# Output copies over two blocks, earlier ranks and row numbers, and a PReLU joined from PSUM, in one FFN

## The chip, the cores and the metric

One NeuronCore of one Trainium2 chip runs the whole program. The metric is the device time of one execution in microseconds (us), taken as the median of several runs. Besides these runs there is one execution under the hardware profiler, from which all rows below come. Engines are named as the profile does: PE is TensorE's matmuls, PEld its weight loads, DVE is VectorE, ACT is ScalarE, POOL is GpSimd, SP is SyncE, which issues most DMAs.

## The reference, cut to what matters

Three stages follow each other, all in float32:

```python
attn = softmax_with_cluster_mask(q, k) @ v          # 2 x 8 heads x 768 x 64
x = attn.transpose(0, 2, 1, 3).reshape(1536, 512)

h = x @ w_in                                        # 512 -> 2048
g = np.maximum(h, 0.0) + alpha * np.minimum(h, 0.0) # PReLU, alpha per column of h
x = g @ w_out                                       # 2048 -> 512

out = x.copy()                                      # then a routed FFN:
e = argmax(x @ w_gate); p = softmax(x @ w_gate)[e]  # 8 experts, one per row
out[x @ w_skip > 0] += p * (relu(x @ w1[e]) @ w2[e])
```

The change lies in the middle stage, the FFN with the PReLU, and in the routing of the first half of its rows.

## The kernel before, in words

Instructions run on each engine in the order in which the Python program emits them (`manual_schedule`); engines wait for each other only through data and through buffers that come free. A float32 product is made from three passes: every operand is split into a rounded high part and a low part (`wh`, `wl` of weights, `xh`, `xl` and `gh`, `gl` of activations), and PE adds high x high, high x low and low x high.

**The FFN** (`ffn`, from L588) works on two halves of the 1536 rows, `gi` = 0 and 1, six row tiles (`GT`) each. In a half a loop runs over 16 blocks `f` of 128 hidden columns. A block has a first layer, `hidden(gi, f)`, and a second layer, `second(gi, f - 1)`, of the block in front of it. The first layer works in two chunks of 384 rows (`c` = 0, 1): PE fills an `h` tile (12 matmuls), a PReLU makes `m` from it, ACT rounds `m` to `gh` (L656) and DVE subtracts to `gl` (L658). The `h` tiles share two PSUM buffers (`ps_h`); ranks (`rk`) and row numbers (`sv`) take their PSUM tiles from the same two. The second layer adds 18 matmuls of 512 columns, three passes over the six row tiles, into six accumulators `ys`. Those are the six buffers of `ps_y`, one PSUM bank each; together with `ps_h` they fill PSUM. The accumulators of half 1 are allotted in `second(1, 0)`, in the first pass over the six tiles, and take over the buffers of half 0 in turn.

**The PReLU** has three forms. The first two blocks of half 0 run beside the last tiles of attention and are made by `blocks()` with `act=True` ("the ACT blocks", four chunks): ACT writes Relu(-h) to `gt` and Relu(h) to `gm`, both from PSUM, and DVE joins them, `gt * nalpha + gm`, with all operands in SBUF (L643 to L645). Half 1 has ACT write Relu(-h), then ACT scale it by `nalpha` (L649, L650), and DVE join max(h, 0) from PSUM with it (L651). The other blocks of half 0 do it on DVE alone (L653, L654). During half 0, weights of later blocks are converted from int64 words by ACT, DVE and POOL (L560 to L568), and POOL makes most `wl`; in half 1 POOL is nearly idle.

**Between the halves** `evac(i)` copies accumulator `i` to SBUF with ACT (L688) and issues two DMAs on SP's queue, to `y1d` and to the output (L689, L690). Three copies are emitted in front of block 0 of half 1 and three behind its first chunk. `after(c)` runs behind each chunk; it also emits set-up constants on DVE and, from block 1, the gate products `gateb` of half 0's rows.

**In half 1's loop** each block first splits weights (`split`: an ACT cast L616 and a DVE subtraction L617), then runs `hidden(1, f)`, then `second(1, f - 1)` up to f = 12 (`TAIL` = 4: the second layers of blocks 12 to 15 come behind the loop, in `tail`). Behind the second layer come steps tied to a block's number: at f = 10 `route1` (choice of the expert, L880 to L890, and running counts `Ms`, L932, all on DVE), at f = 11 `route2` (softmax weight) and `ranks` (three small matmuls `rk`, L940 to L944, which read `M` and `Ms`, then positions on DVE), at f = 12 the first half of `first_tile` (DVE), at f = 13 its second half (six small matmuls `sv`, L968, and `gi0` on DVE) and the gather of rows on POOL's queue. Expert weights are also split here in pieces (`wsp.hi` on ACT, `wsp.lo` on DVE): at f = 6 to 9, and four pieces of a second part at f = 10 and 11.

Of the kernel before, what the change touches and what calls it, by code (L numbers as in the profile page):

```python
# [8 lines left out]
F32 = mybir.dt.float32  # L9
# [6 lines left out]
AF = mybir.ActivationFunctionType  # L16
ALU = mybir.AluOpType
# [3 lines left out]
P = 128  # L21
# [559 lines left out]
def ffn(tc, A, cst, xs, xp, y1d, R, cv, W32, fw, ps_h, cvt, more):  # L581
# [5 lines left out]
    nc = tc.nc  # L587
# [3 lines left out]
    GT = NTT // 2  # L591
    GN = GT * P
    HC = GN // 2
    alpha, nalpha = cst["alpha"], cst["nalpha"]
# [25 lines left out]
    def hidden(gi, f, eng, after, between=lambda: None):  # L620
        for _ in hiddens(gi, f, eng, after, between):
            pass

    def hiddens(gi, f, eng, after=lambda c: None, between=lambda: None, act=False, mid=lambda c: None):
        xh, xl = xs[gi]
        wh, wl = ws.pop((f, 0))
        if gi == 1 and NF - TAIL <= f < NF - 2:
            gh, gl = over["xh"].pop(0), over["xh"].pop(0)
        else:
            gh = fw.tile([P, GN], F32R, tag="gh", name="gh")  # L630
            gl = fw.tile([P, GN], F32R, tag="gl", name="gl")
        for c in range(2):
            o = slice(c * HC, (c + 1) * HC)
            h = ps_h.tile([P, HC], F32, tag="h", name="h")
            for i, (a, x) in enumerate(((wh, xh), (wh, xl), (wl, xh))):
                for k in range(KD):
                    nc.tensor.matmul(h, lhsT=a[:, k * P:(k + 1) * P], rhs=x[:, k, o], start=(k == 0 and i == 0), stop=(k == KD - 1 and i == 2))  # L637
                if i < 2:
                    yield
            m = fw.tile([P, HC], F32, tag="gm", name="gm")  # L640
            if act:
                t = fw.tile([P, HC], F32, tag="gt", name="gt", bufs=1)
                nc.scalar.activation(t, h, AF.Relu, scale=-1.0)  # L643
                nc.scalar.activation(m, h, AF.Relu)
                nc.vector.scalar_tensor_tensor(out=m, in0=t, scalar=nalpha[:, f:f + 1], in1=m, op0=ALU.mult, op1=ALU.add)  # L645
            elif gi == 1:

                t = fw.tile([P, HC], F32, tag="gt", name="gt", bufs=1)
                nc.scalar.activation(t, h, AF.Relu, scale=-1.0)  # L649
                nc.scalar.activation(t, t, AF.Copy, scale=nalpha[:, f:f + 1])  # L650
                nc.vector.scalar_tensor_tensor(out=m, in0=h, scalar=0.0, in1=t, op0=ALU.max, op1=ALU.add)  # L651
            else:
                nc.vector.tensor_scalar(out=m, in0=h, scalar1=0.0, scalar2=alpha[:, f:f + 1], op0=ALU.min, op1=ALU.mult)  # L653
                nc.vector.scalar_tensor_tensor(out=m, in0=h, scalar=0.0, in1=m, op0=ALU.max, op1=ALU.add)  # L654
            mid(c)
            nc.scalar.copy(gh[:, o], m)  # L656
            between()
            eng.tensor_tensor(out=gl[:, o], in0=m, in1=gh[:, o].bitcast(F32), op=ALU.subtract)  # L658
            after(c)
            if c == 1:  # L660
                gs[f] = (gh, gl)
            yield
# [22 lines left out]
    def evac(i):  # L685
        y = ys.pop(i)
        b = wk.tile([P, DM], F32, tag="yb", name="yb", bufs=6)
        nc.scalar.copy(b, y)  # L688
        nc.sync.dma_start(out=y1d[i * P:(i + 1) * P, :DM], in_=b)  # L689
        nc.sync.dma_start(out=A["out"][i * P:(i + 1) * P, :], in_=b)  # L690
        yb[i] = b
# [24 lines left out]
    def route1(t0, nt):  # L716
        ds[t0] = choose(nc, R, wk, LG[:, t0:t0 + nt], t0, nt)
        counts(nc, R, t0, nt)
# [22 lines left out]
    for n, _ in enumerate(blocks()):  # L741
        for _ in range(TODO[n] if n < len(TODO) else 0):
            next(conv2, None)
        if n in SPL:
            f, o = SPL[n]
            split(f, o, nc.gpsimd)
        yield
    wk, ck, ps_y, wsp, slot, last, even, xg, setup = more()
# [4 lines left out]
    for f in range(2, NF):  # L753
        split(f, 1, nc.gpsimd)

        def after(c):
            if c == 0:
                split((f + 1) % NF, 0, nc.gpsimd)
            else:
                convert(f + 2)  # L760
# [21 lines left out]
    for f in range(NF):  # L782
        if f > 0:
            if f < NF - 1:
                split(f + 1, 0, nc.vector)
            split(f, 1, nc.vector, 1)
        if f == 0:
            for i in range(GT // 2):
                evac(i)

        def after(c):
            if f == 0:
                if c == 0:
                    for i in range(GT // 2, GT):
                        evac(i)
                for _ in range(8):
                    next(consts, None)
                return
            for _ in range(2):
                next(consts, None)  # L800
            do(WORK[c])

        def do(n):
            for _ in range(n if f > 0 else 0):
                if work:
                    fn, args = work.pop(0)
                    fn(*args)

        hidden(1, f, nc.vector, after, lambda: do(1))
        if 0 < f <= NF - TAIL:  # L810
            second(1, f - 1)
        if f == 1:
            for c in range(2):
                wsp.load(0, c)
        if f == 2:
            wsp.even[0] = even(0)
        if f == 10:
            route1(0, GT)
        elif f == 11:
            route2(0, GT)  # L820
            for c in range(2, NPC):
                wsp.load(0, c)
            ranks(nc, R, wk, ps_h, 0, GT, "h")
        elif f == 12:
            oh = ck.tile([P, GT, P], F16, tag="ct", name="poh0")
            row0 = first_tile(nc, R, oh, wk, ps_h, "h", GT)
            next(row0)
        elif f == 13:
            next(row0)
            gather_rows(nc, xg, y1d[:GN], R["gi0"])  # L830
        for c, i in ((0, f - 6),) if 6 <= f < 10 else ((1, 2 * f - 20), (1, 2 * f - 19)) if f in (10, 11) else ():

            if i == 0:
                slot()
                wsp.take(0, c)
            wsp.hi(0, c, 512 * i, 512 * (i + 1))
            wsp.lo(0, c, nc.vector, 512 * i, 512 * (i + 1))
            if i == 3:
                wsp.load(1, c)
# [7 lines left out]
    for n in range(GT):  # L847
        i = GT + n
# [15 lines left out]
        if n < 4:  # L864
            c, o = divmod(n, 2)
# [8 lines left out]
def choose(nc, R, wk, lg, t0, nt):  # L874

    M, nd = R["M"], R["nd"]
    ts = slice(t0, t0 + nt)
    l8 = lg[:, :, :NE]
    mx = wk.tile([P, nt], F32, tag="rmx", name="rmx", bufs=1)
    nc.vector.tensor_reduce(out=mx, in_=l8, axis=AX.X, op=ALU.max)  # L880
    nc.vector.tensor_scalar(out=nd[:, ts], in0=lg[:, :, NE], scalar1=0.0, scalar2=FAR, op0=ALU.is_le, op1=ALU.mult)
    d = wk.tile([P, nt, NE], F32, tag="rd8", name="rd8", bufs=1)
    nc.vector.tensor_tensor(out=d, in0=l8, in1=mx.unsqueeze(2).to_broadcast([P, nt, NE]), op=ALU.subtract)

    q = wk.tile([P, nt, NE], F32, tag="rq8", name="rq8", bufs=1)
    nc.vector.scalar_tensor_tensor(out=q, in0=d, scalar=0.0, in1=R["ew"].unsqueeze(1).to_broadcast([P, nt, NE]), op0=ALU.is_equal, op1=ALU.mult)
    m2 = wk.tile([P, nt], F32, tag="rm2", name="rm2", bufs=1)
    nc.vector.tensor_reduce(out=m2, in_=q, axis=AX.X, op=ALU.max)
    nc.vector.tensor_tensor(out=m2, in0=m2, in1=nd[:, ts], op=ALU.add)
    nc.vector.tensor_tensor(out=M[:, ts], in0=q, in1=m2.unsqueeze(2).to_broadcast([P, nt, NE]), op=ALU.is_equal)  # L890
    return d
# [43 lines left out]
def ranks(nc, R, wk, ps, t0, nt, tag):  # L935
    M, Ms = R["M"], R["Ms"]
    ts = slice(t0, t0 + nt)
    rk = ps.tile([P, nt + 1, NE], F32, tag=tag, name="rk")
    rv = rk.rearrange("p t e -> p (t e)")
    nc.tensor.matmul(rv[:, :nt * NE], lhsT=R["tri"], rhs=M[:, ts].rearrange("p t e -> p (t e)"), start=True, stop=False)  # L940
    nc.tensor.matmul(rv[:, :nt * NE], lhsT=R["ones"], rhs=Ms[:, ts].rearrange("p t e -> p (t e)"), start=False, stop=True)
    if t0 == 0:

        nc.tensor.matmul(rk[:, nt], lhsT=R["ones"], rhs=Ms[:, nt], start=True, stop=True)  # L944
        d = wk.tile([P, 1], F32, tag="rdl", name="rdl", bufs=1)
        nc.vector.tensor_scalar(out=d, in0=rk[:, nt, 0:1], scalar1=-1.0, scalar2=float(P), op0=ALU.mult, op1=ALU.add)
        nc.vector.scalar_tensor_tensor(out=d, in0=d, scalar=0.0, in1=R["p0"], op0=ALU.max, op1=ALU.mult)
        nc.vector.tensor_tensor(out=Ms[:, nt, 0:1], in0=Ms[:, nt, 0:1], in1=d, op=ALU.add)
    for step in positions(nc, R, wk, rk[:, :nt], t0, nt):
        step()  # L950
# [689 lines left out]
```

## Time and profile before

| | us |
|---|---|
| median of 3 runs | 743.99 |
| lowest and highest run | 743.09, 745.3 |
| the profiled execution's own time | 744.96 |
| span of the profiled execution, first to last instruction | 743.2 |

The profiled execution is 0.97 us longer than the median, and 1.76 us of it lie outside the span. The rows further down are of two kinds. A row of a group has: line, engine, operation, output<-input, shapes, count, then busy us and mean ns of one, then idle time of the engine in front of the group and what ended it. A row of a timeline has: start in us from the span's start, duration in us, engine, line, operation, output<-input, how many instructions are merged (x), and in brackets the engine's idle time before it with the instruction that ended the wait.

### The profile page before, as it was taken

How to read it: one execution, taken by the hardware profiler on the slowest of the kernel's cores; microseconds unless marked ns; L12 is line 12 of the kernel's file. 1: busy time of each engine (PE TensorE's matmuls, PEld its weight loads, DVE VectorE, ACT ScalarE, POOL GpSimd, SP SyncE). 2: the span in 40 equal slices, each digit the busy share in tenths (PEclk: the TensorE clock that was granted, in tenths of full speed). 3: DMA queues.
4: the chain of work that ended last, by engine and by line, in shares of the span. 5: the costliest groups of instructions: out<-in, count | busy, mean ns of one | idle time of the engine just before them, and what ended most of it. 6: DMA issues, size and time to landing. Idle time of an engine off the chain costs nothing. (4 is left out here: it accounts for less than half of the span.)

```text
span 743.2 us, 11665 instructions
## 1 busy us (share of the span) xinstructions
PE 712.3 (96%) x4030; PEld 625.6 (84%) x4030; DVE 572.1 (77%) x1102; ACT 475.7 (64%) x914; POOL 365.0 (49%) x302
## 2 busy tenths in 40 slices
PE   8999999999999989999999999998989999999993
PEld 5988989988999878888888989988868888888872
DVE  5989888899988888888856899874478877775731
ACT  5879889797899855454536555556427767565630
POOL 4549769678684576666660000000128837482101
PEclk9999999999999999999999999999999999999997
DMA  7967665874663063334107000151629978685000
GB/s 207 228 164 178 130 152 142 198 183 96 155 136 103 0 227 114 114 133 149 73 0 283 1 1 0 58 169 36 235 63 395 395 263 284 254 290 221 17 10 18
DMA packets 45105, 109.21 MB, mean 147 GB/s; under 512 B 9723, under 2 KB 25531, under 8 KB 39665
## 3 DMA queue, kind: packets, MB, share of 16 engines
q1 hardware_dynamic: 38544, 72.01, 34.8%
q0 software_dynamic: 6496, 36.40, 13.4%
q8 instruction: 34, 0.56, 0.3%
q14 instruction: 31, 0.25, 0.1%
HBM read 74.78 MB, written 10.10 MB: 114 GB/s over the span
## 5 line engine op out<-in xcount | busy, mean ns | idle before, releaser
L339 DVE TENSOR_TENSOR etl<-pt,eth 128x384 fp32r<-128x384 f32 x192 | 101.9, 550 | 17.2 <-ACT eth L338 15.0
L338 ACT CAST eth<-pt 128x384 fp32r<-128x384 f32 x192 | 91.2, 489 | 20.5 <-PE pt L336 20.3
L336 PE MATMUL pt<-ident,e 128*128 128x128 f32 x576 | 93.9, 273 | 0.8 <-DVE etl L339 0.7
L318 DVE TENSOR_REDUCE nm<-s 128x1 f32<-128x768 f32 x96 | 90.6, 945 | 3.3 <-PE s L305 3.0
L1110 POOL DMA_INDIRECT xg<-y1d,gi x16 | 27.5, 1718 | 131.2 <-DVE gi L969 115.0
L325 ACT ACTIVATE e<-s,nm 128x768 f32<-128x768 f32 x96 | 87.6, 913 | 5.8 <-DVE nm L318 5.5
L656 ACT CAST gh<-gm 128x384 fp32r<-128x384 f32 x60 | 30.8, 514 | 85.0 <-DVE gm L654 58.9
L336 PEld LDWEIGHTS pt<-ident,e 128*128 128x128 f32 x576 | 73.2, 140 | 8.9 <-DVE etl L339 2.4
L658 DVE TENSOR_TENSOR gl<-gm,gh 128x384 fp32r<-128x384 f32 x60 | 49.9, 832 | 23.3 <-ACT gh L656 23.3
L354 PE MATMUL px<-etl,vh 128*64 128x384 f32 (+1 forms) x192 | 66.0, 370 | 1.7 <-DVE etl L339 1.6
L1374 DVE TENSOR_TENSOR wl<-raw,wh 128x2048 fp32r<-128x2048 f32 (+2 forms) x28 | 48.8, 1755 | 15.5 <-ACT wh L1370 15.5
L637 PE MATMUL h<-xh,wh 128*128 128x384 f32 x256 | 56.6, 343 | 3.7 <-DVE gm L651 3.1
L637 PE MATMUL h<-xh,wl 128*128 128x384 f32 x256 | 56.9, 343 | 1.5 <-DVE wl L617 1.0
L302 PE MATMUL s<-AB 128*128 128x384 f32 x192 | 57.3, 379 | 0.5
L637 PE MATMUL h<-xl,wh 128*128 128x384 f32 x256 | 55.7, 339 | 0.0
L568 POOL TENSOR_TENSOR pre<-ct,pre 128x512 int32<-128x512 int32 x26 | 37.2, 1450 | 36.3 <-DVE ct L566 36.3
L356 PE MATMUL px<-eth,vh 128*128 128x384 f32 x160 | 54.0, 337 | 0.0
L637 PEld LDWEIGHTS h<-xh,wh 128*128 128x128 f32 x256 | 45.7, 189 | 7.4 <-DVE gm L651 3.5
L1232 POOL DMA_INDIRECT out_dram<-o,si x16 | 22.1, 1381 | 60.4 <-DVE o L1227 27.3
L305 PE MATMUL s<-CD 128*128 128x384 f32 x192 | 49.3, 337 | 1.7 <-DMA CD<-st 1.0
L637 PEld LDWEIGHTS h<-xh,wl 128*128 128x128 f32 x256 | 45.0, 190 | 5.0 <-POOL wl L617 3.7
L1370 ACT CAST wh<-raw 128x2048 fp32r<-128x2048 f32 (+2 forms) x28 | 41.3, 1480 | 11.6 <-PE yo L1141 11.6
(337 smaller groups left out, 1831.3 us busy)
## 6 DMA issues: line engine op xcount, KB each, us to landing
AB<-RL SPq DMA_DIRECT2D x32, 384.0 KB, 5.1
raw<-in_wall_dram SPq DMA_DIRECT2D x12, 1024.0 KB, 8.0
raw<-in_w_in_dram SPq DMA_DIRECT2D x16, 512.0 KB, 4.1
raw<-in_w_out_dram SPq DMA_DIRECT2D x16, 512.0 KB, 4.7
Tp<-in_qkT_dram SPq DMA_DIRECT2D x16, 384.0 KB, 3.7
CD<-RL SPq DMA_DIRECT2D x16, 384.0 KB, 6.4
vt<-in_v_dram SPq DMA_DIRECT2D x8, 384.0 KB, 6.2
y1d<-yb SPq DMA_DIRECT2D x12, 256.0 KB, 3.7
```

The lines of the kernel that those rows point to most:

```text
L302: nc.tensor.matmul(s[:, u, :384], lhsT=AB[:, 0, t * P:(t + 1) * P], rhs=AB[:, 1, ks], start=True, stop=False)
L305: nc.tensor.matmul(s[:, u, :384], lhsT=CD[:, 0, t * P:(t + 1) * P], rhs=CD[:, 1, ks], start=False, stop=True)
L318: nc.vector.tensor_reduce(out=nm, in_=s[:, :, :384], axis=AX.XY, op=ALU.max, negate=True)
L325: nc.scalar.activation(e.rearrange("p (u c) -> p u c", u=2), s[:, :, :384], AF.Exp, bias=nm, accum_out=den[:, i % 3:i % 3 + 1])
L336: nc.tensor.transpose(pt[:, i2], e[:, kt * P:(kt + 1) * P], ident)
L338: nc.scalar.copy(eh, pt)
L339: lows[u] = lambda: nc.vector.tensor_tensor(out=etl[:, 3 * u:3 * u + 3, q * P:(q + 1) * P], in0=pt, in1=eh.bitcast(F32), op=ALU.subtract)
L354: nc.tensor.matmul(px[:m], lhsT=vh[:, kt, :m], rhs=etl[:, kt], start=False, stop=False)
L356: nc.tensor.matmul(px, lhsT=vh[:, kt, :], rhs=eth[:, kt], start=False, stop=(kt == NT - 1))
L637: nc.tensor.matmul(h, lhsT=a[:, k * P:(k + 1) * P], rhs=x[:, k, o], start=(k == 0 and i == 0), stop=(k == KD - 1 and i == 2))
L658: eng.tensor_tensor(out=gl[:, o], in0=m, in1=gh[:, o].bitcast(F32), op=ALU.subtract)
L1374: eng.tensor_tensor(out=lo[:, a:b], in0=self.src(t, c)[:, a:b], in1=hi[:, a:b].bitcast(F32), op=ALU.subtract)
```

## The change

- The six output copies of half 0 are spread: two in front of block 0 of half 1, one behind each chunk of block 0, one behind each chunk of block 1.
- `ranks` moves from behind `route2` at f = 11 to right behind `route1` at f = 10.
- `first_tile`'s first half moves from f = 12 to f = 11, its second half from f = 13 to f = 12, between the first layer of block 12 and the second layer of block 11; the gather of rows moves to f = 12.
- The four pieces of the second part of expert weights move from f = 10 and 11 to f = 11 and 12, with their buffer and the load that follows them.
- The ACT blocks use the PReLU of half 1: DVE joins max(h, 0), read from PSUM, with the scaled Relu(-h).

```diff
             m = fw.tile([P, HC], F32, tag="gm", name="gm")
-            if act:
-                t = fw.tile([P, HC], F32, tag="gt", name="gt", bufs=1)
-                nc.scalar.activation(t, h, AF.Relu, scale=-1.0)
-                nc.scalar.activation(m, h, AF.Relu)
-                nc.vector.scalar_tensor_tensor(out=m, in0=t, scalar=nalpha[:, f:f + 1], in1=m, op0=ALU.mult, op1=ALU.add)
-            elif gi == 1:
+            if act or gi == 1:
 
                 t = fw.tile([P, HC], F32, tag="gt", name="gt", bufs=1)
                 nc.scalar.activation(t, h, AF.Relu, scale=-1.0)
...
         if f == 0:
-            for i in range(GT // 2):
+            for i in range(2):
                 evac(i)
 
         def after(c):
+            if f < 2:
+                evac(2 + 2 * f + c)
             if f == 0:
-                if c == 0:
-                    for i in range(GT // 2, GT):
-                        evac(i)
                 for _ in range(8):
                     next(consts, None)
                 return
...
         hidden(1, f, nc.vector, after, lambda: do(1))
+        if f == 12:
+            next(row0)
         if 0 < f <= NF - TAIL:
             second(1, f - 1)
...
         if f == 10:
             route1(0, GT)
+            ranks(nc, R, wk, ps_h, 0, GT, "h")
         elif f == 11:
             route2(0, GT)
             for c in range(2, NPC):
                 wsp.load(0, c)
-            ranks(nc, R, wk, ps_h, 0, GT, "h")
-        elif f == 12:
             oh = ck.tile([P, GT, P], F16, tag="ct", name="poh0")
             row0 = first_tile(nc, R, oh, wk, ps_h, "h", GT)
             next(row0)
-        elif f == 13:
-            next(row0)
+        elif f == 12:
             gather_rows(nc, xg, y1d[:GN], R["gi0"])
-        for c, i in ((0, f - 6),) if 6 <= f < 10 else ((1, 2 * f - 20), (1, 2 * f - 19)) if f in (10, 11) else ():
+        for c, i in ((0, f - 6),) if 6 <= f < 10 else ((1, 2 * f - 22), (1, 2 * f - 21)) if f in (11, 12) else ():
```

## Rows read from the trace of the kernel before

**Rows 1.** The page's first part: busy time, share, instructions of each engine.

```profile
PE 712.3 (96%) x4030; PEld 625.6 (84%) x4030; DVE 572.1 (77%) x1102; ACT 475.7 (64%) x914; POOL 365.0 (49%) x302
```

**Rows 2.** Groups of instructions by line, whole span: the PReLU's operations and the subtraction.

```profile
L658 DVE TENSOR_TENSOR gl<-gm,gh 128x384 fp32r<-128x384 f32 x60 | 49.9, 832 | 23.3 <-ACT gh L656 23.3
...
L650 ACT ACTIVATE gt<-gt,nalpha 128x384 f32<-128x384 f32 x32 | 19.7, 617 | 1.0
...
L649 ACT ACTIVATE gt<-h 128x384 f32<-128x384 f32 x32 | 15.7, 489 | 23.0 <-PE h L637 23.0
...
L654 DVE SCALAR_TENSOR_TENSOR gm<-h,gm 128x384 f32<-128x384 f32 x28 | 15.6, 557 | 1.0
...
L645 DVE SCALAR_TENSOR_TENSOR gm<-gt,nalpha,gm 128x384 f32<-128x384 f32 x4 | 5.3, 1324 | 0.1
```

**Rows 3.** Timeline of DVE in half 0, first PReLU instruction of two successive blocks.

```profile
281.15 0.61 DVE L653 TENSOR_SCALAR gm<-h,alpha 128x384 f32<-128x384 f32 x1
...
289.66 0.61 DVE L653 TENSOR_SCALAR gm<-h,alpha 128x384 f32<-128x384 f32 x1
```

**Rows 4.** Timeline of POOL in the same block.

```profile
283.58 2.89 POOL L617 TENSOR_TENSOR wl<-pre,wh 128x512 fp32r<-128x512 f32 x2
```

**Rows 5.** Timeline of DVE in and behind the ACT blocks.

```profile
253.97 1.36 DVE L645 SCALAR_TENSOR_TENSOR gm<-gt,nalpha,gm 128x384 f32<-128x384 f32 x1
...
271.44 1.28 DVE L566 SCALAR_TENSOR_TENSOR ct<-raw,ct 128x512 int32<-128x512 int32 x2
```

**Rows 6.** Timeline of ACT in the ACT blocks, the first chunk's rounding.

```profile
255.36 0.51 ACT L656 CAST gh<-gm 128x384 fp32r<-128x384 f32 x1 [2.11 <-DVE gm L645]
```

**Rows 7.** Timeline of PE in and behind the ACT blocks: fourth chunk, then block 2.

```profile
258.89 0.97 PE L637 MATMUL h<-xh,wh 128*128 128x384 f32 x4 [0.48 <-ACT gm L644]
...
268.94 0.96 PE L637 MATMUL h<-xh,wl 128*128 128x384 f32 x4 [1.03 <-DVE wl L617]
```

**Rows 8.** Timeline of ACT, blocks 0 and 1 of half 1: copies, casts, rounding.

```profile
395.86 1.56 ACT L688 COPY yb<-y 128x512 f32<-128x512 f32 x3
...
400.02 0.61 ACT L616 CAST wh<-w32a 128x512 fp32r<-128x512 f32 x1
...
404.72 0.51 ACT L656 CAST gh<-gm 128x384 fp32r<-128x384 f32 x1 [0.69 <-DVE gm L651]
```

**Rows 9.** Timeline of DVE, block 0 of half 1: last constant, second chunk's join.

```profile
397.55 0.43 DVE L1432 TENSOR_TENSOR low<-iota 128x256 bf16<-128x256 f32 x1
398.48 0.56 DVE L651 SCALAR_TENSOR_TENSOR gm<-h,gt 128x384 f32<-128x384 f32 x1 [0.51 <-ACT gt L650]
```

**Rows 10.** Timeline of PE: block 1's second chunk, then the second layer's first two passes.

```profile
399.10 0.97 PE L637 MATMUL h<-xh,wh 128*128 128x384 f32 x4 [1.29 <-DVE gm L651]
...
401.31 1.55 PE L673 MATMUL y<-wh,gh 128*128 128x512 f32 x6
402.70 1.53 PE L673 MATMUL y<-wl,gh 128*128 128x512 f32 x6
```

**Rows 11.** Timeline of PE, block 10: last pass of the second layer.

```profile
478.83 1.52 PE L673 MATMUL y<-wh,gl 128*128 128x512 f32 x6
```

**Rows 12.** Timeline of DVE behind block 10: the running counts.

```profile
480.62 1.14 DVE L932 TENSOR_TENSOR Ms<-Ms,M 128x8 bf16<-128x8 bf16 x6
```

**Rows 13.** Timeline of PE: row numbers behind block 13's first layer, then block 14.

```profile
501.15 0.30 PE L968 MATMUL sv<-rs,poh 128*128 128x1 f16 x6
503.28 1.49 PE L637 MATMUL h<-xh,wh 128*128 128x384 f32 x4 [1.83 <-DVE gm L651]
...
507.03 0.86 PE L637 MATMUL h<-xh,wh 128*128 128x384 f32 x4
```

**Rows 14.** Windows: PE, PEld, DVE, ACT, POOL busy, then PEclk, DMA share, GB/s.

```profile
398.00:400.00 2.00, 0.90 (x5) 0.91 (x6) 0.94 (x2) 1.38 (x3) 0.00 (x0) 1.00 1.00 370
...
505.00:507.00 2.00, 2.00 (x8) 2.00 (x7) 0.64 (x2) 0.00 (x0) 1.09 (x1) 0.52 0.08 16
```

**Rows 15.** Timeline of ACT, block 14 of half 1: first chunk's Relu.

```profile
507.29 0.49 ACT L649 ACTIVATE gt<-h 128x384 f32<-128x384 f32 x1 [2.48 <-PE h L637]
```

## The prediction, made before the change was timed

> **What bounds the kernel now.** The page's first part comes first: PE is busy 96% of the span [rows 1], so a gain must come from a wait of PE, or from an engine that paces PE in a stage. The groups by line give the PReLU's prices: the join from SBUF costs 1324 ns on DVE, the one from PSUM 557 [rows 2]. The timelines then show who paces PE where.
>
> In half 0, DVE paces. The first PReLU instruction starts at 281.15 and, one block later, at 289.66 [rows 3]: a period of 8.51 us, which DVE fills with its own work and with waits for ACT's rounding, while POOL makes weights beside it [rows 4]. In the ACT blocks DVE goes from one instruction to the next from 253.97 to 272.72 [rows 5], and ACT stands 2.11 us for DVE's join [rows 6]. PE waits 0.48 us there for an `h` tile, and in block 2 1.03 us for a low part of weights that DVE made late [rows 7].
>
> In half 1, PE paces, but for two waits. ACT makes three accumulator copies in one go behind the first chunk [rows 8], the second chunk's join comes late [rows 9], and PE waits 1.29 us for that `h` tile [rows 10]. Behind block 10's second layer [rows 11] DVE makes the running counts [rows 12], with PE a block away from needing them. Behind block 13's first layer the row numbers take an `h` buffer, so block 14 waits 1.83 us for the other one [rows 13]; the granted clock is then 0.52, the lower level of 1.2 GHz, though after the 1.29 us it had stayed at 1.00, 2.4 GHz [rows 14]. ACT stands idle 2.48 us before block 14's first chunk reaches it [rows 15].
>
> **The PReLU in the ACT blocks: -2.6 us.** Four joins of 1324 ns become four of 557: 4 x 0.767 = 3.07 us of DVE time saved [rows 2]. That the join from PSUM keeps its price beside a busy POOL is seen in half 0: L654 has a PSUM operand and its mean over 28 is 557, although POOL works then [rows 4]; L658, with two SBUF operands, has a mean of 832 [rows 2]. In return ACT scales (617 ns) where it made a second Relu (489): 4 x 0.13 = 0.5 us, which lengthens the way to the join. Net: 3.07 - 0.5 = 2.6. As DVE has no pause from 253.97 to 272.72 and paces the rest of half 0, I count all of that. PE pays a little on the way: the `h` tile is now held until DVE's join, so its wait at 258.89 grows (some 0.5 us by the joins' new places), but what PE waits for behind it, ACT's work and DVE's weights, comes earlier by more. Bounds: 3.07, and nothing.
>
> The Trainium skill (VectorE: DVE Perf Modes, "The perf-mode tier table" and "Rules for kernel authors") speaks against this edit: an operand in PSUM gives at best the slowest rate, which a two-tensor float32 operation has in SBUF too, and for several operations it advises copying out of PSUM first. By it this term would be nothing, and the sum +4.6; the rows show the PSUM form at less than half the price, so I keep -2.6.
>
> **The copies: +3.6 us, and +1.7 from the clock.** One price is given up: behind block 0's first chunk stands one copy (1.56 / 3 = 0.52) instead of three, and ACT is 1.04 earlier. DVE cannot follow so far, since its constants run to 397.55 + 0.43 = 397.98; the join moves from 398.48 to 398.0 [rows 9]. PE's second chunk of block 1 starts at 398.6 instead of 399.1, and second(1, 0) at 400.8 instead of 401.3: -0.5 [rows 10].
>
> But the wait that I see coming is longer. All six accumulators of half 0 must be copied before half 1's can take their banks, in the first pass of second(1, 0). Before, that was done at 395.86 + 1.56 = 397.4 [rows 8], and PE went through the pass without a stop. Now the fifth copy stands behind the first chunk's rounding in block 1, the sixth behind the second chunk's. ACT reaches the casts of block 1 (400.02 is the second [rows 8]) at the same time as before: the 0.5 it won goes to the fourth copy. The fifth copy delays what follows by another 0.4 to 0.5, so the rounding at 404.72 [rows 8] comes at about 405.05; the sixth starts 0.4 later and takes 0.6: done at 406.05. PE has six tiles in a pass of 1.39 us (401.31 to 402.70 [rows 10]): it does four from 400.8, waits for the fifth until 403.3 and for the sixth until 406.1. The second pass starts at 406.3 instead of 402.70: +3.6 net of the 0.5. Queued behind are the rest of the second layer and block 2. From below: even with ACT idle at once, Relu, scaling, join, rounding and copy take about 3 us (0.49 + 0.62 + 0.56 + 0.5 + 0.6 [rows 2, 8]) behind the last matmul, against 1.1 us of PE's work: +2 less 0.5.
>
> PE stands for some 4 us of 4.4 here. After 1.83 us the clock fell, and three groups of four matmuls took 3.75 us (503.28 to 507.03 [rows 13]) where at 2.4 GHz they take 2.1: 1.66 lost. I add 1.66; bounds nothing and twice that.
>
> The SP queue gets six copies' twelve DMAs later, and behind them the loads for blocks 6 on, over 30 us ahead of their use: nothing.
>
> **The ranks: +1.6 us.** They now follow `route1` at once. The second layer's last pass starts at 478.83 [rows 11] and block 11 would start one pass later, at 480.2. The counts end at 480.62 + 1.14 = 481.76 [rows 12]; nothing in the change brings them forward, as they hang on block 10's own second chunk. So PE stands from 480.35 to 481.8, with block 11's first layer queued behind: 1.6. The idle time of 1.45 lies nearer to 1.29, where the clock stayed, than to 1.83, where it fell [rows 13, 14]; I take no fall. Bounds: 1.6 and 1.6 + 1.66.
>
> **The row numbers: -2.3 us.** In front of second(1, 11) the same buffer turn is harmless: 4 us of second layer lie between. The wait of 1.83 and the 1.66 of low clock go, 3.5 together, but ACT comes next: per chunk it has Relu, scaling, a wait for the join, and rounding, and blocks 13 and 14 add two casts each without a second layer as cover. ACT can move up by no more than the 2.48 it stood idle [rows 15], and DVE's joins, which free `h` for block 15, move with it; PE will stand about 1.1 us in front of block 15. The six small matmuls take 0.2 to 0.3 [rows 13] where they now stand. 2.48 - 0.2 = 2.3. Bounds: 0.6 (the clock falls in the new wait) and 3.5.
>
> **Moved at no price.** Two weight pieces per block leave f = 10 and come to f = 12, about 1.3 us of DVE a block (two 512-column operations [rows 5]) and 1.0 of ACT. At f = 12 they take the place of `first_tile`'s DVE work, which goes to f = 11 where the ranks left; second layers hide them. Uncovered, a block would cost 1.3. The gather, alone on POOL's queue, goes out a block earlier; its rows are read in the tail.
>
> **Sum.** -2.6 + 3.6 + 1.66 + 1.6 - 2.3 = +2.0. From the profiled 744.96 that is 746.9; from the median, 0.97 lower, **746.0**. A difference of 0.3%, 2.2 us, is about what a measurement of this kernel can tell from no change: 741.8 to 746.2. My forecast is just inside it.
>
> **Rivals.**
> 1. *Slower: the clock falls in the ranks' wait too.* It decides if 1.45 us are enough. For it: 1.83 were; against: 1.29 were not [rows 13, 14]. +2.0 + 1.66 = +3.6: 747.6. Chance 0.22.
> 2. *Slower: the join from PSUM brings nothing*, because its bank is held longer or the first layer's wait eats it. +4.6: 748.6. Against it: L654's price beside POOL, and DVE without a pause [rows 2, 4, 5]. Chance 0.13. By the Trainium skill's rule named above (VectorE: DVE Perf Modes) it would come out so.
> 3. *No change: the clock stays up or recovers within the stand* at second(1, 0). +0.3: 744.3. Chance 0.13.
> 4. *Faster: the first pass does not wait for the late copies*, so the spreading does what it says and no more (-0.5): -2.6 - 0.5 + 1.6 - 2.3 = -3.8, 740.2. Against it: six live accumulators in six buffers. Chance 0.10.
>
> The forecast has 0.42. Its own spread, about 1 us either way, leaves some 0.25 of that within 0.3% and 0.17 above. With rival 3 and the edges of the others: faster 0.11, same 0.43, slower 0.46. The range, 742.0 to 749.0, leaves out rival 4 and the two highest bounds together.
>
> **What would show it.** DVE's join of the ACT blocks near 557 ns, and block 3 of half 0 some 2.6 us earlier: right; a join above 1 us: wrong. PE waiting for `yb<-y` copies in second(1, 0), over 3 us, with a lower clock behind it: right; no such wait: wrong, and the kernel is faster. PE waiting 1.4 us for `Ms` before block 11, with the clock at 1.00: right. No wait in front of block 14, a new one near 1.1 us for a join in front of block 15: right.

## The result, and the profile after

Over 20 runs of each kernel, the changed kernel takes 748.49 us in the median (747.29 to 750.28), the kernel before 743.92 (742.78 to 749.26). The ratio is 1.0053 with a 95% interval of 1.004 to 1.0065: 3.9 us slower, 3.0 to 4.8; the two medians lie 4.57 apart, within that interval. The forecast was 746.0, +2.0, with a range to 749.0. The profiled execution after took 747.79, with a span of 746.0 against 743.2 before: +2.8. One reason why this pair differs by less than the runs is given further down, under the row numbers.

The page's first part answers [rows 1]: PE is busy 4.2 us longer for the same 4030 matmuls.

```profile
PE 716.5 (96%) x4030; PEld 628.9 (84%) x4030; DVE 570.5 (76%) x1102; ACT 475.9 (64%) x914; POOL 366.5 (49%) x302
```

These 4.2 us are not the change's: 3.0 of them lie ahead of the FFN's first product (242.16 busy instead of 239.13), which comes at 247.15 here and came at 247.19 before. From the first product of half 1 to that of block 2 PE is busy 2.8 longer (15.59 instead of 12.77), from block 13 to the tail 1.6 less (13.08 instead of 14.68), and both of these are in the main the clock, as the windows further down show. Next, the groups by line that answer to [rows 2]. L646 was L651 before and has taken the four chunks of the old L645; numbers behind L640 are 5 or 6 lower now.

```profile
L645 ACT ACTIVATE gt<-gt,nalpha 128x384 f32<-128x384 f32 x36 | 22.2, 617 | 1.2
L646 DVE SCALAR_TENSOR_TENSOR gm<-h,gt 128x384 f32<-128x384 f32 x36 | 20.0, 555 | 24.3 <-ACT gt L645 24.3
```

All 36 joins from PSUM have a mean of 555 ns, the four new ones among them. What became of the DVE time that they save is seen in DVE's timeline behind the ACT blocks, first before (its rows go with [rows 5]), then after:

```profile
270.10 0.75 DVE L562 TENSOR_SCALAR ct<-ct 128x512 f32<-128x512 f32 x2
270.77 0.75 DVE L564 TENSOR_SCALAR ct<-ct 128x512 int32<-128x512 int32 x2
```

```profile
253.96 0.54 DVE L646 SCALAR_TENSOR_TENSOR gm<-h,gt 128x384 f32<-128x384 f32 x1
...
266.94 2.21 DVE L562 TENSOR_SCALAR ct<-ct 128x512 f32<-128x512 f32 x2
269.07 0.75 DVE L564 TENSOR_SCALAR ct<-ct 128x512 int32<-128x512 int32 x2
```

The pair of conversions L562 starts 3.16 us earlier than before, then takes 2.21 us instead of 0.75, and the next pair is only 1.70 earlier (269.07 against 270.77). That 1.7 reaches the end of half 0: the first product of half 1 starts at 389.64 instead of 391.37.

In half 1 the groups of PE's waits name the losses. The columns are: engine, output and line, what it waited for, us in total, times, longest.

```profile
PE y L668 <- ACT yb L683: 3.6, 2, 2.2
...
PE rk L935 <- DVE Ms L926: 1.0, 2, 0.8
```

The first line is new: 3.6 us in which the second layer waits for output copies. PE's timeline shows where, and answers to [rows 10]; the windows (PE, PEld, DVE, ACT, POOL busy, then granted clock, DMA share, GB/s) show the clock.

```profile
398.95 1.09 PE L668 MATMUL y<-wh,gh 128*128 128x512 f32 x4
401.49 0.50 PE L668 MATMUL y<-wh,gh 128*128 128x512 f32 x1 [1.46 <-ACT yb L683]
404.15 0.80 PE L668 MATMUL y<-wh,gh 128*128 128x512 f32 x1 [2.16 <-ACT yb L683]
404.75 2.76 PE L668 MATMUL y<-wl,gh 128*128 128x512 f32 x6
407.31 2.37 PE L668 MATMUL y<-wh,gl 128*128 128x512 f32 x6
409.51 0.88 PE L637 MATMUL h<-xh,wh 128*128 128x384 f32 x4
```

```profile
399.00:401.00 2.00, 1.04 (x5) 0.52 (x3) 1.78 (x6) 1.34 (x4) 0.00 (x0) 1.00 0.50 186
401.00:403.00 2.00, 0.50 (x1) 0.19 (x1) 1.67 (x10) 1.45 (x3) 0.00 (x0) 0.82 0.36 136
403.00:405.00 2.00, 0.85 (x2) 0.75 (x3) 2.00 (x11) 1.51 (x3) 0.00 (x0) 0.50 0.36 134
405.00:407.00 2.00, 2.00 (x6) 1.52 (x6) 1.68 (x5) 0.00 (x0) 0.00 (x0) 0.50 1.12 303
407.00:409.00 2.00, 2.00 (x6) 1.53 (x5) 0.00 (x0) 0.00 (x0) 0.00 (x0) 0.50 0.86 270
409.00:411.00 2.00, 2.00 (x12) 1.90 (x11) 0.58 (x1) 0.62 (x1) 0.00 (x0) 0.98 1.01 406
```

Four of six tiles run, then PE waits for the fifth copy and again for the sixth. The clock falls within this stand (the time in which PE waits), not behind it, and the two passes behind it run at 1.2 GHz (0.50), the second all but its end: 2.76 and 2.37 us where a pass had taken 1.53 [rows 10]. The second pass starts 2.05 later than before (404.75 against 402.70), block 2 4.08 later (409.51 against 405.43).

Last, PE's timeline around the ranks and the row numbers, which answers to [rows 13]:

```profile
484.71 0.18 PE L934 MATMUL rk<-M,tri 128*128 128x48 bf16 x1 [0.27 <-DVE M L884]
485.69 0.18 PE L935 MATMUL rk<-Ms,ones 128*128 128x48 bf16 x1 [0.80 <-DVE Ms L926]
...
498.49 0.30 PE L962 MATMUL sv<-rs,poh 128*128 128x1 f16 x6
...
512.37 0.97 PE L637 MATMUL h<-xh,wh 128*128 128x384 f32 x4 [0.86 <-DVE gm L646]
```

The ranks stand in front of block 11, which starts at 485.91 instead of 480.19: 5.72 late where block 10 was 4.08 late, so +1.64. The row numbers run without a wait; block 14 starts at 507.02 without one either, and a wait of 0.86 stands in front of block 15. From block 13's start to the tail it is 13.94 us (502.83 to 516.77) instead of 16.51 (496.96 to 513.47).

### The profile page after: what moved, and what is told of

Its sections match the earlier page's. It is cut to its first block, busy times and chain, and to the rows that moved or that the text cites. A ratio compares the mean times of both kernels' runs of the same rounds, so it can differ in the third digit from the quotient of the medians.

```text
span 746.0 us, 11665 instructions
## 1 busy us (share of the span) xinstructions
PE 716.5 (96%) x4030; PEld 628.9 (84%) x4030; DVE 570.5 (76%) x1102; ACT 475.9 (64%) x914; POOL 366.5 (49%) x302
## 5 line engine op out<-in xcount | busy, mean ns | idle before, releaser
L1104 POOL DMA_INDIRECT xg<-y1d,gi x16 | 23.9, 1496 | 130.3 <-DMA raw<-in_wall_dram 114.1
L651 ACT CAST gh<-gm 128x384 fp32r<-128x384 f32 x60 | 30.8, 514 | 81.9 <-DVE gm L649 59.8
```

## The experiments

**Each part alone.** Four kernels make one part of the change each, in the kernel before.

The PReLU:

```diff
-            if act:
...
-            elif gi == 1:
+            if act or gi == 1:
```

> Only the PReLU of the ACT blocks is changed, all else as before. Theory: DVE paces half 0, the four joins fall from 1324 to about 550 ns, but DVE's conversion for block 3 then meets POOL's last attention work and gives part back: half 1 starts 1.7 us earlier than before, time -1.7 us (ratio 0.9977). Rival one (the prediction's own sum): nothing is given back, -2.6 us. Rival two (an operand in PSUM brings nothing): within 0.5 us of before, and joins above 1 us.

Ratio to before 0.9977 (0.9953 to 1.0001), 743.16 us over 12 runs: about -1.7, in an interval from -3.5 to +0.1. From the first product of the FFN to the first one of half 1 it is 142.5 us (247.74 to 390.27), against 144.2 before (247.2 to 391.4) and 142.5 after. The pair L562 is slow here too. DVE's timeline:

```profile
267.49 2.20 DVE L562 TENSOR_SCALAR ct<-ct 128x512 f32<-128x512 f32 x2
```

By the trace the part is worth 1.6 to 1.7 us by itself, so the shortfall belongs to it and not to its neighbours in the change.

The copies:

```diff
-            for i in range(GT // 2):
+            for i in range(2):
                 evac(i)
...
+            if f < 2:
+                evac(2 + 2 * f + c)
             if f == 0:
-                if c == 0:
-                    for i in range(GT // 2, GT):
-                        evac(i)
```

> Only the six output copies are spread over blocks 0 and 1 of half 1. Theory: PE stands for the fifth and sixth copy in the first pass of the second layer, the second pass starts 3.6 to 3.8 us later than before counted from the start of half 1, and the clock falls to its lower level and takes 1 to 2 us more: +4.8 to +5.8 us in all. Rival: the copies are not waited for, -0.5 us. Second rival: the wait is there and the clock stays up, +3.7 us.

Ratio 1.0081 (1.0053 to 1.011), 752.08 us over 7 runs: about +6.0 (+3.9 to +8.2), more than the whole change costs and a little more than expected. PE's timeline has the two waits, and the first product of block 2:

```profile
403.80 0.51 PE L673 MATMUL y<-wh,gh 128*128 128x512 f32 x1 [1.45 <-ACT yb L688]
406.46 0.79 PE L673 MATMUL y<-wh,gh 128*128 128x512 f32 x1 [2.15 <-ACT yb L688]
407.05 2.76 PE L673 MATMUL y<-wl,gh 128*128 128x512 f32 x6
409.61 2.68 PE L673 MATMUL y<-wh,gl 128*128 128x512 f32 x6
412.13 0.88 PE L637 MATMUL h<-xh,wh 128*128 128x384 f32 x4
```

Half 1 starts at 391.94 here, so block 2 comes 20.19 us behind it; before, 405.43 - 391.37 = 14.06. The difference of 6.1 agrees with the runs.

The ranks:

```diff
             route1(0, GT)
+            ranks(nc, R, wk, ps_h, 0, GT, "h")
...
-            ranks(nc, R, wk, ps_h, 0, GT, "h")
```

> Only the ranks move to block 10. Theory: PE stands 1.4 to 1.5 us for the running counts in front of block 11, the clock stays at its upper level there, +1.6 us. Rival one: the clock falls in this wait too, +3.3 us. Rival two: block 11's later work absorbs it, 0.

Ratio 1.0002 (0.9984 to 1.002), 745.57 us over 12 runs. PE's timeline and two windows:

```profile
481.72 0.18 PE L940 MATMUL rk<-M,tri 128*128 128x48 bf16 x1 [0.28 <-DVE M L890]
482.70 0.18 PE L941 MATMUL rk<-Ms,ones 128*128 128x48 bf16 x1 [0.80 <-DVE Ms L932]
...
505.93 0.98 PE L637 MATMUL h<-xh,wh 128*128 128x384 f32 x4 [1.83 <-DVE gm L651]
```

```profile
484.00:486.00 2.00, 2.00 (x14) 2.00 (x13) 1.86 (x7) 0.61 (x2) 0.00 (x0) 1.00 0.00 0
...
507.00:509.00 2.00, 2.00 (x13) 2.00 (x12) 1.28 (x4) 1.03 (x3) 1.36 (x1) 1.00 0.00 0
```

The stand is there with its full 1.64 us, and the clock stays at 1.00 behind it (first window), yet the runs show next to nothing, +1.5 at most. The last window points to one reason: in this execution the clock did not fall behind block 14's wait of 1.83, though the wait is the same as in [rows 13], where it fell. What runs lose to the clock can be estimated as span x (1 - mean granted clock): 5.8 us a run in this kernel, 6.5 in the kernel before. With span x clock in place of the span, the medians are 738.17 and 736.71: +1.46, near the stand. This is an estimate only: the loss varies by 1.6 to 1.8 us from run to run, so a difference of 0.7 between 12 runs and 30 is not clear of noise, and that the clock alone hides the stand from the runs is not shown.

The row numbers, their gather and the weight pieces (the pieces stand in blocks 10 and 12 here, since the ranks stay in block 11):

```diff
+        if f == 12:
+            next(row0)
...
-        elif f == 13:
-            next(row0)
+        elif f == 12:
             gather_rows(nc, xg, y1d[:GN], R["gi0"])
```

> Only the row numbers move in front of block 12's second layer, with the gather and with the first half of their DVE work in block 11; the four weight pieces stand in blocks 10 and 12. Theory: PE's wait of 1.8 us in front of block 14 and the low clock behind it go, ACT paces blocks 13 to 15 instead and PE waits about 0.9 us in front of block 15: -2.3 us from an execution in which the clock fell before, less from one in which it did not. Rival: ACT does not pace, all of 3.5 us goes. Second rival: the move is hidden by the tail, 0.

Ratio 0.9989 (0.997 to 1.0007), 744.13 us over 12 runs: about -0.8, in an interval that holds no change. PE's timeline:

```profile
493.19 0.29 PE L968 MATMUL sv<-rs,poh 128*128 128x1 f16 x6 [0.96 <-DVE gm L651]
...
507.05 0.97 PE L637 MATMUL h<-xh,wh 128*128 128x384 f32 x4 [0.83 <-DVE gm L651]
```

Block 11 holds both the ranks and the row numbers' first half on DVE here, and block 12's join is late, which costs 0.96 that the whole change does not pay. Block 14's wait is gone and the one before block 15 is 0.83. From block 13 to the tail it is 13.9 us. The kernel with the ranks alone, whose clock stayed up, takes 15.0 for it, the kernel before, whose clock fell, 16.5. So by the traces this part is worth some 2.4 us where the clock would have fallen (16.5 - 13.9, less 0.2 for the six small matmuls that now stand in front of block 13) and some 0.9 where not.

**The copies undone in two ways.** The changed kernel, with all copies made around block 0's chunks:

```diff
-            if f < 2:
-                evac(2 + 2 * f + c)
             if f == 0:
+                evac(2 + 2 * c)
+                evac(3 + 2 * c)
```

> The changed kernel with the copies still spread, but all behind block 0: two in front, two behind each of its chunks, none in block 1. Theory: what costs is that the last two copies stand behind block 1's chunks; here PE does not wait for a copy in the second layer's first pass and no low clock follows it. PE waits about 1.1 to 1.3 us for block 1's second chunk, as before the change. The time falls by 4.5 to 5.5 us against the changed kernel, to about 1 us below the kernel before (ratio 0.9985). Rival: banks of the accumulators come free late for another reason, the wait stays, ratio 1.005 as in the changed kernel.

Ratio to before 0.9969 (0.9955 to 0.9982), 742.42 us over 12 runs. PE's timeline has no wait for a copy, the second pass 1.38 us behind the first, and a wait of 0.80, not 1.1 to 1.3, in front of block 1's second chunk:

```profile
397.50 0.97 PE L637 MATMUL h<-xh,wh 128*128 128x384 f32 x4 [0.80 <-DVE gm L646]
...
399.70 1.55 PE L668 MATMUL y<-wh,gh 128*128 128x512 f32 x6
401.08 1.53 PE L668 MATMUL y<-wl,gh 128*128 128x512 f32 x6
```

And with all six in front of block 0:

```diff
-            for i in range(2):
+            for i in range(GT):
                 evac(i)
...
-            if f < 2:
-                evac(2 + 2 * f + c)
```

> The changed kernel with all six copies in front of block 0. Theory: ACT stood idle 1.7 us there before block 0's first chunk was ready, so the copies cost nothing, PE waits only for DVE's constants in front of block 1's second chunk (about 0.7 us), and no low clock follows: 0.5 us below the version with all copies behind block 0, ratio to the kernel before 0.998. Rival: ACT becomes late for block 0 and PE's wait in front of block 1's second chunk stays at 1.3 us or grows: no gain over that version.

Ratio 0.997 (0.9954 to 0.9986), 742.63 us over 11 runs. PE's timeline:

```profile
396.21 0.96 PE L637 MATMUL h<-xh,wh 128*128 128x384 f32 x4 [0.68 <-DVE gm L646]
```

Either way some 6.2 us come back, from +3.9 to about -2.3, more than was expected of the first of the two. The two copies left for block 1 cost more than the whole loss of the change. The 0.5 us that six copies in front were to win over copies around block 0's chunks did not come: the runs show no difference between the two, and the traces 0.12 (from half 1's start to its second layer 9.32 against 9.44).

**The clock by itself.** The changed kernel, with 16 matmuls of 384 columns into a tile that nothing reads, in the two stands:

```diff
+                    if gi == 1 and t == 4:
+                        dm = ps_h.tile([P, HC], F32, tag="h", name="dm")
+                    if gi == 1 and t >= 4:
+                        for _ in range(5 if t == 4 else 11):
+                            nc.tensor.matmul(dm, lhsT=a[:, :P], rhs=w[:, :HC], start=True, stop=True)
                     ys[gi * GT + t] = ps_y.tile([P, DM], F32, tag="y", name="y")
```

> The changed kernel with 16 extra matmuls of 384 columns, whose result is not used, in PE's wait for the fifth and sixth copy: 5 in front of the fifth accumulator's first matmul, 11 in front of the sixth's. They fit into the waits of 1.5 and 2.2 us. Theory: the 2 us that the second and third pass took longer come from the lower clock alone; with PE busy the clock stays at 1.00, the passes take 1.4 us each, and the time falls by 1.5 to 2 us against the changed kernel, ratio to the kernel before 1.0025 to 1.003. Rival: the passes are slow for another reason (DMA traffic, DVE), the time stays at ratio 1.005 or rises by the added work.

Ratio to before 1.0033 (1.0017 to 1.0049), 747.2 us over 12 runs, against 1.0053: some 1.5 us faster, but the two intervals overlap (up to 1.0049 here, from 1.004 there), so the trace has to show it. PE's timeline, and the window behind the stand:

```profile
399.69 1.09 PE L673 MATMUL y<-wh,gh 128*128 128x512 f32 x4
...
404.87 0.50 PE L673 MATMUL y<-wh,gh 128*128 128x512 f32 x1 [0.23 <-ACT yb L688]
405.21 1.56 PE L673 MATMUL y<-wl,gh 128*128 128x512 f32 x6
406.61 1.54 PE L673 MATMUL y<-wh,gl 128*128 128x512 f32 x6
407.99 0.87 PE L637 MATMUL h<-xh,wh 128*128 128x384 f32 x4
```

```profile
405.00:407.00 2.00, 2.00 (x9) 1.63 (x10) 2.00 (x7) 0.34 (x1) 0.00 (x0) 1.00 0.70 246
```

The sixth tile starts 5.18 us behind the first here (404.87 - 399.69) and 5.20 in the changed kernel (404.15 - 398.95): the copies come no earlier. Block 2 follows the first tile by 8.30 instead of 10.56. So in this execution these 2.3 us were the clock alone, and work that nobody needs won them back.

**Why the PReLU gave 1.7 and not 2.6.** POOL's attention operations run beside the slow pair L562. Two kernels, the changed one and the one before, leave out POOL's addition and scaling of the attention output for the last three row tiles:

```diff
-        return [
+        return ([
             lambda: pl(out=xa, in0=xa, in1=xb, op=ALU.add),
             lambda: pl(out=xa, in0=xa, in1=rb, op=ALU.mult),
+        ] if (n, g) != (len(seq) - 1, 1) else []) + [
```

> The changed kernel without two of POOL's operations for the last three row tiles of attention (the sum of its two parts and the division by the softmax sum; that part of the FFN's input for half 1 is left unscaled). Theory: the PReLU saved 2.8 us less 0.4, and 1.4 of it was given back because DVE's first conversion pair for block 3 ran beside POOL's last attention operations (2.21 us instead of 0.75); without the two operations POOL is done earlier, the pair takes 0.75, and from the first layer's first matmul to the start of half 1 it takes 141.0 to 141.3 us instead of 142.5. Rival: DVE is not what counts behind the ACT blocks, 142.5 stays.

> The kernel before without the same two POOL operations. Theory: DVE's conversion pair did not meet POOL there, so little is won: from the first layer's first matmul to the start of half 1 it takes 143.5 to 144.2 us instead of 144.2, and the difference to the changed kernel without them grows to 2.5 to 3 us from 1.7. Rival: POOL paced the ACT blocks before too, and both kernels win the same 1.4 us.

From the FFN's first product to half 1, the changed kernel takes 141.28 us without them (248.63 to 389.91) and 142.49 with them; the kernel before 143.55 without (248.67 to 392.22) and 144.2 with. The PReLU is worth 2.27 where POOL is less busy, against 1.7. DVE's timeline of the changed kernel without POOL's operations:

```profile
268.31 0.93 DVE L563 TENSOR_SCALAR ct<-ct 128x512 f32<-128x512 f32 x2
```

Of the kernel before without them, the second conversion of the pair:

```profile
271.24 0.43 DVE L563 TENSOR_SCALAR ct<-ct 128x512 f32<-128x512 f32 x1 [0.69 <-ACT ct L561]
```

Of POOL in the changed kernel itself:

```profile
266.68 1.02 POOL L408 TENSOR_TENSOR xh<-xa,zero 128x384 fp32r<-128x384 f32 x1
267.78 1.08 POOL L409 TENSOR_TENSOR xl<-xa,xh 128x384 fp32r<-128x384 f32 x1
```

The pair takes 2.21 us beside these two operations, 0.93 where they had run before it, 0.75 in the kernel before, where it starts 0.34 after the last one. So the slow pair is POOL's doing: by these two single executions 0.5 to 0.6 of the missing 0.9 come back. The difference was expected to grow to 2.5 to 3; why the other 0.3 did not come stays open. Part of the 2.27 comes by way of ACT, which is late for the conversion in the kernel before (0.69) and not in the changed one. The two single times, 749.79 and 743.98, say nothing on this, since both kernels reach the FFN 1.5 us later.

The Trainium skill (SBUF — State Buffer, "SBUF: two separate sides") says that VectorE and GpSimd share one pair of SBUF ports, held for a whole instruction, by VectorE for a two-tensor SBUF operation or a fast single-source one. The trace agrees: the two conversions take 1.05 and 1.24 us, and each ends 0.29 us behind one of POOL's two operations (267.99 against 267.70, 269.15 against 268.86).

**A version that beats both.** The kernel before with the PReLU, all six copies in front of block 0, its constants 2 and 14 behind the two chunks instead of 8 and 8, the ranks between block 11's two layers, the row numbers between block 12's, half of the one-hot rows on POOL, and the weight pieces in blocks 10 and 12:

```diff
-            for i in range(GT // 2):
+            for i in range(GT):
                 evac(i)
...
-                for _ in range(8):
+                for _ in range(14 if c else 2):
                     next(consts, None)
...
+        if f == 11:
+            ranks(nc, R, wk, ps_h, 0, GT, "h")
+        if f == 12:
+            next(row0)
...
-    places(nc.vector, R, oh, 0, nt)
+    places(nc.gpsimd, R, oh, 0, nt // 2)
+    places(nc.vector, R, oh, nt // 2, nt)
```

> The kernel before with the parts that paid: PReLU joined from PSUM in the ACT blocks, all six copies in front of block 0, only two constants behind its first chunk, ranks between the layers of block 11 and row numbers between the layers of block 12, half of the one-hot rows on POOL, weight pieces in blocks 10 and 12. Theory: -1.7 (PReLU), -1.3 (no wait for block 1's second chunk), -0.9 to -2.4 (row numbers, by whether the clock fell), no ranks' wait: -4 to -5.4 us, ratio 0.9935 to 0.995. Rival: the parts get in each other's way on DVE in block 11 and give back 1 us or more, ratio above 0.996.

Ratio 0.9938 (0.9917 to 0.9959), 740.3 us over 5 runs: 4.6 us faster than before. In PE's timeline the ranks and the row numbers run without a wait; of the waits of half 1 that this study is about only the one before block 15 is left:

```profile
481.55 0.18 PE L933 MATMUL rk<-M,tri 128*128 128x48 bf16 x1
...
489.98 0.30 PE L962 MATMUL sv<-rs,poh 128*128 128x1 f16 x6
...
503.87 0.97 PE L637 MATMUL h<-xh,wh 128*128 128x384 f32 x4 [0.83 <-DVE gm L646]
```

## Why the prediction was right, and where its sizes were off

The direction of every part, and the waits that were to appear and vanish, came out as written; the time lies inside the range, 2.5 us above the forecast. It is outside the 0.3% that the forecast still lay in, and nearer to rival 1 (747.6) and rival 2 (748.6): by the time alone they could not be told from the prediction, and it is the traces that rule them out.

**The PReLU, -2.6: mis-sized, -1.7.** The joins came down as predicted, four of 0.54 to 0.56, and rival 2 falls. It was the Trainium skill's rule (VectorE: DVE Perf Modes, "The perf-mode tier table"), by which the edit brings nothing; the runs show 555 ns from PSUM beside POOL, against 1324 from SBUF [rows 2]. A PSUM operand did not make this operation slower. Nor is SBUF the slow place by itself. In half 1, with POOL idle, the kernel before has an operation of the same kind with both tensors in SBUF:

```profile
L712 DVE SCALAR_TENSOR_TENSOR junk<-yb,raw 128x512 f32<-128x512 f32 x48 | 31.8, 686 | 0.1
```

It takes 686 ns for 512 columns, where the SBUF join took 1324 for 384 with POOL at work beside all four. So the gain is that the join no longer pays for POOL, and where POOL is idle no gain of this size is to be expected.

The step that failed is "As DVE has no pause from 253.97 to 272.72 and paces the rest of half 0, I count all of that". That reading was wrong in one place, since DVE did pause there once, 0.58 us for ACT's rounding:

```profile
264.95 1.41 DVE L658 TENSOR_TENSOR gl<-gm,gh 128x384 fp32r<-128x384 f32 x1 [0.58 <-ACT gh L656]
```

That is not what cost the 0.9, for the work behind the joins did start 3.16 earlier. But being earlier put it beside POOL's last attention operations, which had been over before. The price of an instruction was taken from a place to which it no longer belonged: its 0.75 became 2.21. Of 2.6, 1.7 stayed.

**The copies, +3.6: right, 3.78.** Half 1 starts 1.73 early and the second pass 2.05 late, 3.78 together. The stand begins behind the fourth tile and has the two steps predicted, 1.46 and 2.16 = 3.62 us where "some 4 us" stood. What the spreading won is as predicted: the wait in front of block 1's second chunk is 0.67 instead of 1.29, for a forecast of 0.5. Rival 4, no wait, falls with the timeline; it was wrong because the six buffers of the accumulators have no spare.

**The clock behind it, +1.66: mis-sized, 2.03.** Taken from the fall behind block 14's wait, where it comes back within three groups. Here it falls inside the stand and both passes behind it are slow: block 2 is 4.08 late where the second pass was 2.05. The run with unused matmuls gives 2.3 for it. Rival 3, in which the clock stays up, is out.

**The ranks, +1.6: right in the traces, 1.64; not seen in the runs.** The stand came as two short waits, 0.27 and 0.80, with small matmuls between, and the kernel with the ranks alone shows 1.00 in the window behind it, as the changed kernel's trace does (window 487 to 489): rival 1 is out for these two executions. The runs of this part alone show +0.1, and the estimate by the clock that would bring back the rest is not clear of noise. The counts end where the prediction had them, behind block 10's own second chunk.

**The row numbers, -2.3: right for the profiled pair, -2.4, and by an estimate about -1.2 over the runs.** ACT's pace came next as written, with a wait of 0.86 before block 15 where "near 1.1" stood. What the prediction took for a fixed part of the kernel before, the low clock behind block 14, is not one: in the profiled executions it fell in three (before, the PReLU alone, the copies alone) and stayed up in two (the ranks alone, and the kernel before without POOL's operations), each time behind the same 1.83. Windows of the PReLU alone and of the kernel before without POOL's operations:

```profile
503.00:505.00 2.00, 2.00 (x8) 2.00 (x7) 1.52 (x4) 0.71 (x2) 1.36 (x1) 0.50 0.00 0
```

```profile
505.00:507.00 2.00, 2.00 (x13) 2.00 (x12) 1.47 (x4) 1.07 (x3) 1.36 (x1) 1.00 0.00 0
```

So the kernel before pays it only at times, and removing it gains less. The part alone lost 6.1 us a run to the clock where the kernel before lost 6.5: some 0.4 in the mean, not 1.66, an estimate with an error of its own size.

**Moved at no price: right.** Block 11 is 5.72 us late, block 12 5.71 (494.30 against 488.59) and block 13 5.87 (502.83 against 496.96), so the weight pieces, the first half of the row numbers and the gather cost PE nothing there, and the 0.17 are the six small matmuls.

**The sum.** In the profiled pair, with measured terms: -1.7 + 3.8 + 2.0 + 1.6 - 2.4 = +3.3 at the tail's start, of which the tail gives 0.5 back (from its first product to the end 229.2 us instead of 229.7, not pursued): +2.8. Over the runs the row numbers would bring some 1.2 less: +4.0, where +3.9 was measured. Since that 1.2 is an estimate and the other terms come from one pair of executions, an agreement to 0.1 is luck; what the experiments show is that the copies and the clock behind them are the loss.

## What to carry to other kernels

Before spreading work that frees a buffer, find the first instruction that needs the last buffer: here six accumulators in six buffers were all wanted within one pass, and two copies moved behind it in ACT's order cost 6 us to shorten a wait of 1.29 to 0.67. Before moving an operand to another memory, see what runs beside it: here a busy POOL, and not SBUF, made the join dear. Time saved on an engine that paces a stage is gained in full only if what it runs next costs the same at its new place; look at what the other engines do there. A stand of PE costs its length and then the clock behind it, and the second half has to be read from several executions, since one profile shows only one draw.

## What the runs showed of the hardware

- The clock behind one and the same wait of 1.83 us differs from execution to execution: 0.52 and 0.50 in windows behind it before [rows 14] and with the PReLU alone, 1.00 with the ranks alone and in the kernel before without POOL's operations. The stand of 1.46 + 2.16 us lowered it in all three profiled executions that left it unfilled and in which the windows or the lengths of the passes were read (the change, the copies alone, the change without POOL's operations).
- 16 matmuls with no reader, 3.3 us of PE in a stand of 3.6, kept the clock at 1.00 and won 2.3 us in the trace; the runs show 1.5 (ratio 1.0033 against 1.0053), with overlapping intervals.
- A float32 operation on DVE with one SBUF input was slowed by a busy POOL too, not only one with two: 0.75 us for a pair of conversions of 512 columns became 2.21, while the join with one operand in PSUM kept its 0.55.
